# The third weight matrix of a gated MLP converted after the attention instead of during it

## The chip, the cores and the metric

One core of a Trainium2 chip. The metric is the device time of one execution in microseconds (us). The five engines run their own instruction streams: PE (TensorE; PEld is its weight load), DVE (VectorE), ACT (ScalarE), POOL (GpSimd) and SP, which only issues DMAs here. 1% of this kernel's time is 7.9 us.

## The reference, cut to what matters

Three stages, each feeding the next: a masked attention, a gated MLP over all tokens, and a routed mixture of eight experts.

```python
scores = scale * q @ k.T                      # B, H, S, D = 4, 8, 576, 64
scores = where(mask_local if h < 4 else mask_strided, scores, -1e9)
x = softmax(scores) @ v                       # -> 2304 tokens x 512

gate = 1 / (1 + exp(-(x @ w_gate)))           # 512 x 1536
x = (gate * (x @ w_val)) @ w_out              # w_out: 1536 x 512

e_idx = argmax(x @ w_gate2)                   # 8 experts, 512 -> 1024 -> 512
out = x + p * (relu(x @ w1[e_idx]) @ w2[e_idx])   # only where x @ w_skip > 0
...
```

## The kernel before, in words

**Products in three.** Each operand of the large products is held as a high and a low part, and a product is three matmuls (L434 high by high, L435 high by low, L436 low by high). The MLP's weights arrive as 64-bit words. A matrix of a group of 256 hidden columns is two pieces of 512 KB, each fetched by one DMA from SP and converted (`Weights.convert`) by five DVE operations on 128x512 elements (L396, L399, L402, L405, L409), then a copy on ACT that makes the high part (L417), then a subtraction on POOL that makes the low part (L413). The piece's matmuls need both parts. Tiles are named by matrix: `wg`, `wv`, `wo` the raw words, `cvg`, `cvv`, `cvo` the scratch, `whg`/`wlg` and so on the parts. The MLP runs in groups of hidden columns; group 0 is the one that the change touches.

**Attention.** 32 sub-items run as a software pipeline of steps t = 0 to 34. What a step issues, and in which order, is written out by hand as a string of letters, `ORDER`; its first string serves t < 14, the second t = 14 to 32. The letters that matter: S scores (PE L281), e/E exponentials (ACT), I inverse of the sums (DVE L312, L313), n/N normalisation (POOL L319, tile `sm`), f/F transposition (PE L328 of `sm`, evacuated by DVE L330 or ACT L332), A the product with v (PE L342, evacuated by ACT L350/L362 and DVE L351/L364), m/M row maximum (DVE L297), G one piece of filler, L loads. D is `drain(1)`, which issues the next one of the queued conversion operations; a and p issue the ACT copy and the POOL subtraction of a piece whose five operations are done. The raw piece is fetched in the steps listed in `FETCH`, and its conversion is queued two steps later, piece after piece in the order of `early`.

**Filler.** Half products of group 0 for the first three units of 512 tokens (`gv_raw`, six matmuls each, 24 halves) fill PE: one half a step from step `FILL0` on, what is left in the last step.

**The turn.** After the attention its memory is reused by other pools. Then come `glu_raw` of units 0 and 1 (ACT L506 sigmoid, DVE L507 product, ACT L509 copy, POOL L510 subtraction), the gate and value products of unit 3 (`gv(0, 3)`, with ACT L462, DVE L463, ACT L464, DVE L467), and the output products `mout(0, u)`: these alone use `wo` of group 0, three matmuls with its first piece, three with its second, then an ACT copy (L526). `ticks` between them converts the next groups' matrices.

**End of the last group.** At its last unit, `route` is called after each third of the last gate and value products ("g" or "v", kk = 0 to 3) and issues parts of the routing of the unit before: `turn_back` (PE, DVE L738), then the nine small DVE operations of `pick` (L747 to L775), and at ("v", 3) `prep`, which transposes expert 0's first gathered rows (PE L872, ACT L874, DVE L876) for the first expert products (PE L998).

Of the kernel before, what the change touches and what calls it, by code (L numbers as in the profile page):

```python
# [21 lines left out]
def kernel(  # L22
# [25 lines left out]
    G = 2  # L48
# [9 lines left out]
    NU = -(-NT // UT)  # L58
# [114 lines left out]
    def load_qk(b, ty, hp):  # L173
        if hp == 0:
            r = [att.tile([128, 2, 4, 2, D], F32, tag="raw", bufs=4, name=f"raw_{n}{b}{ty}") for n in "qk"]
            r.append(att.tile([128, 2, 2, D], F32, tag="rem", bufs=2, name=f"rem{b}{ty}"))
            raw_t[b, ty] = r
        r = raw_t[b, ty]
        h0 = 4 * ty + 2 * hp
        for i, src in enumerate((q, k)):  # L180
            for h in range(2):
                nc.sync.dma_start(
                    r[i][:, hp, :, h, :], src[b, h0 + h, 0:512, :].rearrange("(p r) d -> p r d", r=4)
                )
        for i, src in enumerate((q, k)):
            nc.sync.dma_start(
                r[2][64 * hp:64 * hp + 64, i], src[b, h0:h0 + 2, 512:S, :].rearrange("h p d -> p h d")
            )
# [234 lines left out]
    after_act, after_pool, glus = [], [], []  # L423

    def flush(jobs):
        todo = list(jobs)
        jobs.clear()
        for job in todo:
            job()

    wt = {}
# [6 lines left out]
    def run(steps, n=99):  # L438
        for _ in range(n):
            if next(steps, 0) == 0:  # L440
                return
# [4 lines left out]
    def gv_mm(g, u, f, nm, tag, step=None):  # L446
        fs = slice(128 * f, 128 * f + 128)
        ps = bank([128, width(u)], tag)
        assert wt[g, nm].ready == 2
        whi, wlo = wt[g, nm].hi, wt[g, nm].lo  # L450
        for kk in range(KD):
            mm3(ps, whi[:, kk, fs], wlo[:, kk, fs], plane(xth[u], kk), plane(xtl[u], kk), kk == 0, kk == KD - 1)
            if step is not None:
                step(nm, kk)
        return ps

    def glu(g, u, f, pg, pvl):
        n = width(u)
        gt = slab2([128, 2, n], F32R, f"gt{g}{u}{f}")
        gts.setdefault((g, u), []).append(gt)  # L460
        sg = late.tile([128, UT], F32, tag="sg", bufs=2, name="sg")[:, 0:n]
        nc.scalar.activation(sg, pg, AF.Sigmoid)  # L462
        nc.vector.tensor_tensor(sg, sg, pvl, op=ALU.mult)  # L463
        nc.scalar.copy(gt[:, 0, :], sg)  # L464

        def low_part():
            nc.vector.tensor_tensor(gt[:, 1, :], sg, gt[:, 0, :].bitcast(F32), op=ALU.subtract)  # L467

        flush(glus)
        if f + 1 < G:  # L470
            glus.append(low_part)
        else:
            low_part()

    def gv_f(g, u, f, step=None):
        glu(g, u, f, *(gv_mm(g, u, f, nm, "ZY"[f], step) for nm in "gv"))

    def gv(g, u):
        for f in range(G):
            gv_f(g, u, f)  # L480

    def gv_raw(u, f, i):
        if i == 0:
            raws[u, f] = slab([128, 2, UT], F32, f"gvr{u}{f}")
        ps = bank([128, UT], "Z")
        w = wt[0, "gv"[i]]
        assert w.ready == 2
        fs = slice(128 * f, 128 * f + 128)
        for kk in range(KD):
            mm3(ps, w.hi[:, kk, fs], w.lo[:, kk, fs], plane(xth[u], kk), plane(xtl[u], kk), kk == 0, kk == KD - 1)  # L490
            if kk == 1:
                yield
        dst = raws[u, f][:, i, :]
        if i == 0:
            nc.vector.tensor_copy(dst, ps)
        else:
            nc.scalar.copy(dst, ps)  # L497
        yield

    def glu_raw(u):  # L500
        for f in range(G):
            raw = raws.pop((u, f))
            gt = slab2([128, 2, UT], F32R, f"gt0{u}{f}")
            gts.setdefault((0, u), []).append(gt)
            sg = raw[:, 0, :]
            nc.scalar.activation(sg, sg, AF.Sigmoid)  # L506
            nc.vector.tensor_tensor(sg, sg, raw[:, 1, :], op=ALU.mult)  # L507
            yield
            nc.scalar.copy(gt[:, 0, :], sg)  # L509
            nc.gpsimd.tensor_tensor(gt[:, 1, :], sg, gt[:, 0, :].bitcast(F32), op=ALU.subtract)  # L510
            yield
# [31 lines left out]
    load_qk(0, 1, 0)  # L543
    load_v(0, 0)
    load_qk(0, 1, 1)
    for nm in "gvo":
        wt[0, nm] = Weights(0, nm, slab, slab)
    ADD = 20
    NRAW = 3
    FILL = {}  # L550
    FILL0 = 13
    BUSY = ((1, 2), (1, 2), (1, 2), (1, 2), (0, 1), (0, 1), (0, 1), (0, 1), (0, 1), (0, 0), (0, 1), (0, 1), (1, 1), (1, 1), (0, 1), (1, 0))
    FETCH = (5, 6, 7, 8, 13, 14)
    halves = [x for u in range(NRAW) for i in range(2) for f in range(G) for x in [gv_raw(u, f, i)] for _ in range(2)]
    for i, x in enumerate(halves):
        FILL.setdefault(min(FILL0 + i, NS + 2), []).append(x)
    early = [(nm, i) for nm in "gvo" for i in range(2)]
    turn(items[0], 0, 8)
    turn(items[0], 1, 1)
    cq = []  # L560
# [59 lines left out]
    def step_loads(t):  # L620
# [16 lines left out]
        if 17 <= t < 23:  # L637
            late_consts(t - 17)
        if t in FETCH:
            nm, i = early[FETCH.index(t)]  # L640
            wt[0, nm].fetch(i)
        if t - 2 in FETCH:
            nm, i = early[FETCH.index(t - 2)]
            cq.append(wt[0, nm].convert(i))
# [7 lines left out]
        "D": lambda t: drain(1), "a": lambda t: flush(after_act), "p": lambda t: flush(after_pool),  # L652
    }
    ps_of = {}
    ORDER = ("eSfEmIFnGaNDTMRpDADL", "SmeEfTIanGNDMRDpLDAF", "GAeEInNfFapDDDD")
    for t in range(NS + 3):
        for c in ORDER[(t >= 14) + (t >= NS + 1)]:
            steps_of[c](t)
# [10 lines left out]
    def slab2(shape, dt, name):  # L669
        return late.tile(shape, dt, tag="slab2", bufs=NSLAB2, name=name)  # L670
# [160 lines left out]
    def init_xs(u):  # L831
        if u == 0:
            zero.append(late.tile([128, TW], F32, tag="row", bufs=8, name="zero"))
            nc.gpsimd.memset(zero[0], 0.0)
            nc.gpsimd.memset(zero[0][:, TW - 1:TW].bitcast(I32), 1 << 16)
        for i in range(3 * u, min(3 * u + 3, NE * SLOTS // 128)):
            nc.sync.dma_start(xs[128 * i:128 * i + 128, :], zero[0])
# [46 lines left out]
    def plan(g, nm):  # L884
        w = Weights(g, nm, slab2, slab3)
        wt[g, nm] = w
        conv.extend([(w, 0), (w, 1)])
# [19 lines left out]
    for g in range(1, NG):  # L907
        for nm in "gvo":
            plan(g, nm)
    todo = [glu_raw(u) for u in range(NRAW)]  # L910
    for n in range(2 * G):
        for u in range(2):
            run(todo[u], 1)
    gv(0, NRAW)
    for u in range(NU):

        def between(d, u=u):
# [7 lines left out]
    for g in range(1, NG):  # L925
        last = g == NG - 1
        for u in range(NU):
            if g == 2:
                init_xs(u)
            if not last:  # L930
                gv_f(g, u, 0)
                if u > 0:
                    mout(g, u - 1, ticks)
                elif g > 1:
                    mout(g - 1, NU - 1, ticks)
                gv_f(g, u, 1)
                continue
            steps = back = picks = iter(())

            def seat(nm, kk):  # L940
                nonlocal steps
                if u > 1 and (nm, kk) == ("g", 1):
                    steps = place(u - 2, rank_sums(rst[u - 2][1], "X"))
                run(steps, 1)

            gv_f(g, u, 0, seat)
            run(steps)
            if u == 0:
                w_e0.append(load_e(0, 0))
            if u == NU - 1:  # L950
                xg, ins = fetch(0, PARTS[:1])
                tc.add_to_no_dep_group("head", ins.ins)
            if u > 0:
                mout(g, u - 1, part(u - 1))
                back = turn_back(u - 1)
                picks = pick(u - 1)
            else:
                mout(g - 1, NU - 1, ticks)

            def route(nm, kk):  # L960
                if u == NU - 1 and (nm, kk) == ("v", 3):
                    pp.extend(prep(0, xg, PARTS[:1], tag="Z", gates=False))
                if nm == "g":
                    run(back, 2)
                else:
                    run(picks, 4)

            gv_f(g, u, 1, route)
            run(picks)
            for i in {0: (1, 2), 1: (3, 4), 2: (5, 6), 3: (7,)}.get(u, ()):  # L970
                w_e0.append(load_e(0, i))
# [15 lines left out]
    pending, jobs = [], []  # L987
# [297 lines left out]
```

## Time and profile before

| | us |
|---|---|
| median of 3 runs | 789.06 (784.98 to 790.59) |
| profiled execution, its own time | 785.84 |
| its span in the trace | 784.1 |

Granted TensorE clock over the span: 0.994 of full speed. The profile is of one execution; the times below are us from the start of its span. Busy time counts no waits. A matmul's start is recorded, its end is modelled, so starts are what is compared.

### The profile page before, as it was taken

What the parts mean: (1) busy time and instruction counts of PE and PEld (TensorE: products, weight loads), DVE (VectorE), ACT (ScalarE), POOL (GpSimd) and SP (SyncE); (2) the same over time, 40 slices, a digit from 0 to 9 for tenths busy, and PEclk for the clock granted to TensorE, in tenths of its full rate; (3) what the DMA queues carried; (4) which work ended last, traced back from release to release, by engine and by line L of the source; (5) the groups of instructions that cost most, each with busy time, mean ns of one, the idle gap of its engine ahead of it and who ended that gap; (6) DMA issues with size and microseconds to landing.
All of it is one profiled execution on the core that took longest, in us unless ns stands there. A gap on an engine that the chain in (4) does not pass through costs nothing. (4 is left out here: it accounts for less than half of the span.)

```text
span 784.1 us, 12866 instructions
## 1 busy us (share of the span) xinstructions
PE 757.9 (97%) x4522; PEld 629.0 (80%) x4524; DVE 487.9 (62%) x1130; ACT 345.2 (44%) x1001; POOL 261.6 (33%) x259
## 2 busy tenths in 40 slices
PE   8989999999999999999999999999999999999994
PEld 5757677688888888888888888888888888888882
DVE  4698876469465574575466457277775776665650
ACT  5877679565211221222111212344444755666530
POOL 5565643253111011011011101424424456665610
PEclk9999999999999999999999999999999999999998
DMA  6988451213101333011002000223346766666600
GB/s 162 212 208 220 105 117 32 81 28 108 54 29 52 110 96 122 28 54 54 27 28 81 28 27 27 71 97 135 109 145 185 254 231 234 233 234 207 215 28 13
DMA packets 86447, 87.82 MB, mean 112 GB/s; under 512 B 55991, under 2 KB 58551, under 8 KB 86376
## 3 DMA queue, kind: packets, MB, share of 16 engines
q1 hardware_dynamic: 81032, 76.45, 32.4%
q0 software_dynamic: 3616, 7.33, 2.7%
q10 hardware_dynamic: 1728, 3.15, 1.1%
q8 instruction: 38, 0.62, 0.4%
q14 instruction: 33, 0.27, 0.1%
HBM read 73.48 MB, written 19.28 MB: 118 GB/s over the span
## 5 line engine op out<-in xcount | busy, mean ns | idle before, releaser
L435 PE MATMUL psX<-gt,who 128*128 128x512 f32 (+1 forms) x240 | 88.4, 369 | 0.0
L434 PE MATMUL psX<-gt,who 128*128 128x512 f32 (+1 forms) x240 | 88.4, 368 | 0.0
L464 ACT CAST gt<-sg 128x512 fp32r<-128x512 f32 (+1 forms) x54 | 30.9, 572 | 130.3 <-DVE sg L463 128.8
L436 PE MATMUL psX<-gt,wlo 128*128 128x512 f32 (+1 forms) x240 | 88.3, 368 | 0.0
L319 POOL TENSOR_TENSOR sm<-sm,rs 96x384 f32<-96x384 f32 (+2 forms) x64 | 51.0, 816 | 66.4 <-DVE rs L313 37.0
L528 DVE TENSOR_TENSOR acc<-psX,acc 128x512 f32<-128x512 f32 (+1 forms) x100 | 62.8, 631 | 11.6 <-PE psX L436 11.4
L463 DVE TENSOR_TENSOR sg<-sg,psZ 128x512 f32<-128x512 f32 (+1 forms) x27 | 17.0, 628 | 67.4 <-PE psZ L436 65.8
L413 POOL TENSOR_TENSOR wlv<-cvv,whv 128x512 fp32r<-128x512 f32 x12 | 17.0, 1415 | 113.9 <-ACT whv L417 113.9
L436 PEld LDWEIGHTS psX<-gt,wlo 128*128 128x128 f32 x240 | 45.2, 188 | 7.6
L434 PEld LDWEIGHTS psX<-gt,who 128*128 128x128 f32 x240 | 45.2, 189 | 7.5
L435 PEld LDWEIGHTS psX<-gt,who 128*128 128x128 f32 x240 | 45.2, 188 | 7.5
L434 PE MATMUL psZ<-xth,whv 128*128 128x512 f32 (+1 forms) x132 | 50.3, 381 | 0.9 <-ACT gvr L497 0.7
L434 PE MATMUL psZ<-xth,whg 128*128 128x512 f32 (+1 forms) x132 | 50.3, 381 | 0.0
L436 PE MATMUL psZ<-xth,wlv 128*128 128x512 f32 (+1 forms) x132 | 49.2, 373 | 0.0
L435 PE MATMUL psZ<-xtl,whv 128*128 128x512 f32 (+1 forms) x132 | 49.1, 372 | 0.0
L436 PE MATMUL psZ<-xth,wlg 128*128 128x512 f32 (+1 forms) x132 | 49.0, 371 | 0.0
L435 PE MATMUL psZ<-xtl,whg 128*128 128x512 f32 (+1 forms) x132 | 49.0, 371 | 0.0
L463 DVE TENSOR_TENSOR sg<-sg,psY 128x512 f32<-128x512 f32 (+1 forms) x27 | 17.0, 628 | 47.9 <-PE psY L436 45.7
L1076 POOL DMA_INDIRECT out_dram<-xg x16 | 21.1, 1321 | 75.1 <-DVE xg L1075 40.4
L413 POOL TENSOR_TENSOR wlo<-cvo,who 128x512 fp32r<-128x512 f32 x12 | 17.4, 1450 | 83.4 <-ACT who L417 83.4
L467 DVE TENSOR_TENSOR gt<-sg,gt 128x512 fp32r<-128x512 f32 (+1 forms) x54 | 34.0, 630 | 17.1 <-ACT gt L464 16.6
L413 POOL TENSOR_TENSOR wlg<-cvg,whg 128x512 fp32r<-128x512 f32 x12 | 18.4, 1531 | 71.8 <-ACT whg L417 55.2
(748 smaller groups left out, 2244.5 us busy)
## 6 DMA issues: line engine op xcount, KB each, us to landing
w1r<-in_moe_w_dram SPq DMA_DIRECT2D x32, 512.0 KB
w2r<-in_moe_w_dram SPq DMA_DIRECT2D x32, 512.0 KB
wg<-in_moe_w_gate_dram SPq DMA_DIRECT2D x12, 512.0 KB
wv<-in_moe_w_val_dram SPq DMA_DIRECT2D x12, 512.0 KB
wo<-in_moe_w_out_dram SPq DMA_DIRECT2D x12, 512.0 KB
raw_q<-in_q_dram SPq DMA_DIRECT2D x32, 128.0 KB
raw_k<-in_k_dram SPq DMA_DIRECT2D x32, 128.0 KB
xs<-zero SPq DMA_DIRECT2D x14, 260.5 KB
```

The costliest lines, as they stand in the source:

```text
L319: nc.gpsimd.tensor_tensor(x, x, rs[:n, h, 0:m].rearrange("p (w o) -> p w o", o=1).to_broadcast([n, m, c]), op=ALU.mult)
L413: nc.gpsimd.tensor_tensor(l, wf, h.bitcast(F32), op=ALU.subtract)
L434: nc.tensor.matmul(ps, lhsT=whi, rhs=xhi, start=start, stop=False)
L435: nc.tensor.matmul(ps, lhsT=whi, rhs=xlo, start=False, stop=False)
L436: nc.tensor.matmul(ps, lhsT=wlo, rhs=xhi, start=False, stop=stop)
L463: nc.vector.tensor_tensor(sg, sg, pvl, op=ALU.mult)
L464: nc.scalar.copy(gt[:, 0, :], sg)
L467: nc.vector.tensor_tensor(gt[:, 1, :], sg, gt[:, 0, :].bitcast(F32), op=ALU.subtract)
L528: nc.vector.tensor_tensor(ac, po, ac, op=ALU.add)
L1076: nc.gpsimd.indirect_dma_start(out=out[:, :], out_offset=bass.IndirectOffsetOnAxis(ap=xg[t][:n, TW - 1:TW].bitcast(I32), axis=0), in_=y, i ...
```

## The change

`wo` of group 0 leaves the attention. Its two pieces are fetched behind the attention, into tiles of the pools that open there, and its ten conversion operations are issued one by one by a callback of the gate and value products of unit 3 (each call also issues the waiting POOL and ACT parts). In the attention a step up to 13 drains two conversion operations instead of three, the four pieces left are fetched at steps 5, 6, 8, 10, the filler starts at step 14 instead of 13, and at the end of the last group `prep` is called at ("v", 0) instead of ("v", 3).

```diff
-    for nm in "gvo":
+    for nm in "gv":
         wt[0, nm] = Weights(0, nm, slab, slab)
...
-    FILL0 = 13
+    FILL0 = 14
...
-    FETCH = (5, 6, 7, 8, 13, 14)
+    FETCH = (5, 6, 8, 10)
...
-    early = [(nm, i) for nm in "gvo" for i in range(2)]
+    early = [(nm, i) for nm in "gv" for i in range(2)]
...
-    ORDER = ("eSfEmIFnGaNDTMRpDADL", "SmeEfTIanGNDMRDpLDAF", "GAeEInNfFapDDDD")
+    ORDER = ("eSfEmIFnGaNDTMRpDAL", "SmeEfTIanGNDMRDpLDAF", "GAeEInNfFapDDDD")
...
     todo = [glu_raw(u) for u in range(NRAW)]
+    wt[0, "o"] = Weights(0, "o", slab2, slab3)
+    for i in range(2):
+        wt[0, "o"].fetch(i)
+    first_o = chain(wt[0, "o"].convert(0), wt[0, "o"].convert(1))
+
+    def turn_o(nm, kk):
+        flush(after_pool)
+        flush(after_act)
+        run(first_o, 1)
+
     for n in range(2 * G):
         for u in range(2):
             run(todo[u], 1)
-    gv(0, NRAW)
+    for f in range(G):
+        gv_f(0, NRAW, f, turn_o)
+    for jobs in (after_act, after_pool):
+        flush(jobs)
...
-                if u == NU - 1 and (nm, kk) == ("v", 3):
+                if u == NU - 1 and (nm, kk) == ("v", 0):
                     pp.extend(prep(0, xg, PARTS[:1], tag="Z", gates=False))
```

Conversion operations that the attention's steps issue: before, three a step in steps 8 to 13 and 2, 1, 3, 3, 3 in steps 14 to 18, 30 in all; after, two a step in steps 8 to 13 and 3, 3, 2 in steps 14 to 16, 20 in all.

DVE around step 12, before. L396 to L409 are the conversion, `cvv` and `wv` the value matrix, the other rows the attention's own:

```order
L399 SCALAR_TENSOR_TENSOR cvv_918<-wv_659,cvv_918 128x512
L330 COPY pT<-psY 128x288
L297 TENSOR_REDUCE mx<-psX 126x2
L312 TENSOR_SCALAR sums<-sums 96x6
L313 RECIPROCAL rs<-sums 96x6
L402 SCALAR_TENSOR_TENSOR cvv_918<-wv_659,cvv_918 128x512
L230 TENSOR_SCALAR kq_983<-psY 128x32x16
L297 TENSOR_REDUCE mx<-psX 126x2
L405 TENSOR_SCALAR wv_659<-wv_659 128x512
L351 TENSOR_TENSOR xtl_381<-psY,xth_379 128x160
L351 TENSOR_TENSOR xtl_922<-psY,xth_920 128x128
L409 SCALAR_TENSOR_TENSOR cvv_918<-wv_659,cvv_918 128x512
```

The same place after (`cvg`, `wg`: the gate matrix):

```order
L312 TENSOR_SCALAR sums<-sums 96x6
L313 RECIPROCAL rs<-sums 96x6
L405 TENSOR_SCALAR wg_583<-wg_583 128x512
L230 TENSOR_SCALAR kq_975<-psY 128x32x16
L297 TENSOR_REDUCE mx<-psX 126x2
L409 SCALAR_TENSOR_TENSOR cvg_834<-wg_583,cvg_834 128x512
L351 TENSOR_TENSOR xtl_381<-psY,xth_379 128x160
L351 TENSOR_TENSOR xtl_916<-psY,xth_914 128x128
```

The conversion operation that stood last in the step, behind L351, is gone, and the conversion as a whole is one matrix further back.

DVE at the turn, before (`gvr` the raw products of `glu_raw`, `sg`/`gt` those of unit 3, the last row the next group's conversion):

```order
L507 TENSOR_TENSOR gvr_1804<-gvr_1804 128x512
L463 TENSOR_TENSOR sg<-sg,psZ 128x512
L463 TENSOR_TENSOR sg<-sg,psY 128x512
L467 TENSOR_TENSOR gt_2525<-sg,gt_2525 128x512
L467 TENSOR_TENSOR gt_2556<-sg,gt_2556 128x512
L396 TENSOR_SCALAR cvg_2579<-wg_2573 128x512
```

and after:

```order
L507 TENSOR_TENSOR gvr_1859<-gvr_1859 128x512
L396 TENSOR_SCALAR cvo_2487<-wo_2457 128x512
L399 SCALAR_TENSOR_TENSOR cvo_2487<-wo_2457,cvo_2487 128x512
L402 SCALAR_TENSOR_TENSOR cvo_2487<-wo_2457,cvo_2487 128x512
L405 TENSOR_SCALAR wo_2457<-wo_2457 128x512
L409 SCALAR_TENSOR_TENSOR cvo_2487<-wo_2457,cvo_2487 128x512
L396 TENSOR_SCALAR cvo_2510<-wo_2459 128x512
L399 SCALAR_TENSOR_TENSOR cvo_2510<-wo_2459,cvo_2510 128x512
L402 SCALAR_TENSOR_TENSOR cvo_2510<-wo_2459,cvo_2510 128x512
L463 TENSOR_TENSOR sg<-sg,psZ 128x512
L405 TENSOR_SCALAR wo_2459<-wo_2459 128x512
L409 SCALAR_TENSOR_TENSOR cvo_2510<-wo_2459,cvo_2510 128x512
```

All ten operations of `wo` now stand behind the last L507, eight of them ahead of the first L463 and two between the two L463.

DVE at the end of the last group, before:

```order
L771 TENSOR_REDUCE rmx<-eq 128x4
L773 TENSOR_TENSOR eq<-eq,rmx 128x32
L775 TENSOR_TENSOR oh_all<-eq,va 128x32
L876 TENSOR_TENSOR xx_6072<-psZ,xx_6072 128x2x128
L876 TENSOR_TENSOR xx_6073<-psZ,xx_6073 128x2x128
L463 TENSOR_TENSOR sg<-sg,psY 128x256
L467 TENSOR_TENSOR gt_6084<-sg,gt_6084 128x256
```

and after:

```order
L876 TENSOR_TENSOR xx_6038<-psZ,xx_6038 128x2x128
L876 TENSOR_TENSOR xx_6039<-psZ,xx_6039 128x2x128
L747 TENSOR_TENSOR lg<-lp 128x40
L759 TENSOR_REDUCE rmx<-lg 128x4
L761 TENSOR_SCALAR va<-lg 128x4
L763 TENSOR_TENSOR eq<-lg,rmx 128x32
L765 TENSOR_TENSOR lm_all<-lg,rmx 128x32
L767 TENSOR_TENSOR eq<-eq,desc 128x32
L771 TENSOR_REDUCE rmx<-eq 128x4
L773 TENSOR_TENSOR eq<-eq,rmx 128x32
L775 TENSOR_TENSOR oh_all<-eq,va 128x32
L463 TENSOR_TENSOR sg<-sg,psY 128x256
```

The two L876, which wait for the gathered rows, now stand ahead of the nine operations of `pick` instead of behind them.

## Rows read from the trace of the kernel before

**Rows 1.** The page's first part: busy us, share of the span, instructions.
```profile
PE 757.9 (97%) x4522; PEld 629.0 (80%) x4524; DVE 487.9 (62%) x1130; ACT 345.2 (44%) x1001; POOL 261.6 (33%) x259
```

**Rows 2.** Busy by stretch: length, PE PEld DVE ACT POOL, clock, DMA, GB/s.
```profile
34.35:60.80 26.45, 22.84 (x230) 16.43 (x228) 23.69 (x60) 20.85 (x97) 16.01 (x17) 1.00 0.89 215
60.80:75.20 14.40, 13.88 (x121) 10.29 (x120) 11.54 (x30) 9.20 (x47) 10.42 (x13) 1.00 0.95 245
75.20:96.80 21.60, 19.67 (x166) 14.67 (x164) 18.23 (x46) 15.98 (x70) 12.07 (x16) 0.92 0.50 117
91.70:95.20 3.50, 3.50 (x18) 2.94 (x17) 2.52 (x13) 2.24 (x13) 2.34 (x4) 0.51 0.01 2
580.00:600.00 20.00, 17.67 (x140) 15.72 (x140) 13.91 (x67) 10.57 (x32) 7.20 (x14) 1.00 0.66 220
```

**Rows 3.** Waits of PE, first 100 us: total, count, median.
```profile
PE psY L328 <- POOL sm L319: 3.2, 5, 1.2
```

**Rows 4.** Busy by stretch, DVE's conversion alone: first tile wg, then tile wo.
```profile
34.35:60.80 26.45, 6.45 (x10) 1.00 0.89 215
75.20:96.80 21.60, 8.06 (x9) 0.92 0.50 117
```

**Rows 5.** PE's timeline: start, us, instruction; steps 3 and 8, then step 13's filler.
```profile
17.09 0.90 PE L281 MATMUL psX<-kq 64*96 64x128 f32 x12
...
34.80 0.90 PE L281 MATMUL psX<-kq 64*96 64x128 f32 x12
...
57.65 0.48 PE L434 MATMUL psZ<-xth,whg 128*128 128x512 f32 x1
...
59.13 0.39 PE L167 MATMUL psY<-busy_in 128*128 128x512 bf16 x1
```

**Rows 6.** PE's timeline at the turn.
```profile
153.40 0.78 PE L342 MATMUL psY<-pT,v 108*64 108x108 f32 x12
...
166.27 0.39 PE L436 MATMUL psX<-gt,wlo 128*128 128x512 f32 x1
```

**Rows 7.** DVE's timeline at the turn and behind it.
```profile
159.53 2.40 DVE L507 TENSOR_TENSOR gvr<-gvr 128x512 f32<-128x512 f32 x2 [1.27 <-ACT gvr L506]
163.17 0.69 DVE L463 TENSOR_TENSOR sg<-sg,psZ 128x512 f32<-128x512 f32 x1 [1.24 <-ACT sg L462]
...
183.35 0.42 DVE L396 TENSOR_SCALAR cvv<-wv 128x512 int32<-128x512 int32 x1
...
185.14 1.53 DVE L405 TENSOR_SCALAR wv<-wv 128x512 int32<-128x512 int32 x1
...
187.32 0.42 DVE L396 TENSOR_SCALAR cvo<-wo 128x512 int32<-128x512 int32 x1
...
194.63 0.69 DVE L409 SCALAR_TENSOR_TENSOR cvo<-wo,cvo 128x512 f32<-128x512 int32 x1
```

**Rows 8.** POOL's timeline behind the turn.
```profile
184.61 1.78 POOL L413 TENSOR_TENSOR wlv<-cvv,whv 128x512 fp32r<-128x512 f32 x1 [2.79 <-ACT whv L417]
...
196.06 1.49 POOL L413 TENSOR_TENSOR wlo<-cvo,who 128x512 fp32r<-128x512 f32 x1 [1.75 <-ACT who L417]
```

**Rows 9.** DVE's timeline at the end of the last group.
```profile
579.54 0.20 DVE L747 TENSOR_TENSOR lg<-lp 128x40 f32<-128x40 f32 x1
...
580.89 0.19 DVE L775 TENSOR_TENSOR oh_all<-eq,va 128x32 bf16<-128x32 f32 x1
...
582.37 0.41 DVE L463 TENSOR_TENSOR sg<-sg,psY 128x256 f32<-128x256 f32 x1
...
583.25 0.43 DVE L467 TENSOR_TENSOR gt<-sg,gt 128x256 fp32r<-128x256 f32 x1 [0.47 <-ACT gt L464]
```

**Rows 10.** PE's timeline at the same place: transposes and first expert product.
```profile
580.33 0.66 PE L872 MATMUL psZ<-ident,xg 128*128 128x128 f32 x4
582.18 0.39 PE L998 MATMUL psY<-xx,w100h 128*128 128x256 f32 x1 [1.20 <-DVE xx L876]
```

**Rows 11.** Tile xg, 560 to 590 us: what its engine idled for before it.
```profile
  DMA xg<-xs: 0.2, 1
```

## The prediction

> **What bounds the kernel now.** I read the page's busy shares first: PE works 97% of the span, 757.9 of 784.1 us [rows 1]. Only what lets PE idle, or runs it at half clock, can be won or lost, some 26 us. So the second view is the busy time by stretch, cut at the steps that the change touches [rows 2]. In steps 8 to 13 (34.35 to 60.80) PE is busy 22.84 of 26.45 us, in steps 14 to 16 13.88 of 14.40, in steps 17 to 20 19.67 of 21.60, and at the end of the last group 17.67 of 20. In the first of these DVE is the busiest engine, 23.69 us, with fixed order and the conversions in it. The waits of PE there name POOL, though: 3.2 us in five waits on the normalisation L319 [rows 3]. POOL's operand comes from DVE's inverses, so a lighter DVE helps only in part. Last I read the timelines at the turn and at the end of the last group [rows 6 to 11], where the change puts new work.
>
> The sum is made against the profiled execution, 785.84 us (784.1 of span and 1.7 around it). The median of the runs is 789.06, 3.2 above; I add these 3.2 at the end.
>
> **Steps 8 to 13.** Eighteen conversion operations become twelve. Ten of them cost DVE 6.45 us there, 0.645 each [rows 4], so six fewer free 3.9 us of DVE. The floor is the pace of steps 3 to 7, which convert nothing: the scores of step 3 start at 17.09, of step 8 at 34.80 [rows 5], 17.71 / 5 = 3.54 a step, 21.3 for six; 26.45 - 21.3 = 5.2 is the most that can go. Nothing goes if POOL sets the pace. The waits on POOL lie between, 3.2, near to DVE's own 3.9; I take -3.3, bounds -5.2 and 0.
>
> **Filler.** Step 13's half takes 57.65 to 59.13 = 1.48 us of PE [rows 5], in a step that DVE sets, so it was free. It now stands at the end, after the attention, where PE has no gap to put it in: +1.5.
>
> **Steps 14 to 16.** Eight operations instead of six: 2 x 0.645 = 1.3 of DVE. But PE idles only 0.5 us in these 14.40 us and DVE has 2.9 us free [rows 2]. Value +0.4, bounds 0 and 1.3.
>
> **Steps 17 to 20.** Nine operations of `wo` leave, 8.06 us of DVE [rows 4]. They were slow there, 0.9 each. PE idles 21.60 - 19.67 = 1.9 us in the stretch and runs 91.70 to 95.20 at 0.51 of its clock, the lower of its two levels, 1.2 GHz [rows 2], which loses 3.50 x 0.49 = 1.7. With DVE at 10 instead of 18 of 21.60 us I take both, -3.6, which is also the most; the other bound is -1.5 (three quarters of the idle time, and the clock as before). What is late next is PE itself.
>
> **The turn.** This is the main price. In the trace PE's first three matmuls of `mout(0, 0)` need the first piece of `wo`, the next three the second, and the sixth, which needs the last low part, starts at 166.27 [rows 6]. Now all ten operations stand on DVE behind the last L507, which ends at 159.53 + 2.40 = 161.93 [rows 7]. A piece took 183.35 to 187.32 = 3.97 from its first operation to the next piece's first, with one operation held up: an L405 of 1.53 us instead of 0.42, while POOL ran L413 from 184.61 to 186.39 [rows 7, 8]. At the turn POOL is busy with L510 in the same way, so I take one held-up operation a piece. Two pieces are 7.9, one L463 between them 0.6 (0.69, overlapping a little): DVE is done at 170.5. Behind the last operation come the ACT copy and the POOL subtraction: from L409's end at 194.63 + 0.69 = 195.32 to L413's end at 196.06 + 1.49 = 197.55 is 2.23 [rows 7, 8]. So the sixth matmul starts at 172.7 instead of 166.27: +6.4. PE's order has nothing else to do meanwhile, and everything that follows it on PE moves by as much. Without a held-up operation each piece is 1.1 shorter, +4.2; with two each, +8.6.
>
> What queues behind the wait: on DVE the two L463 and L467 of unit 3 and then the next group's conversion start some 6 us late, but PE is as late, so nobody waits for them more than before. The fetches cost nothing: 512 KB at the 215 GB/s of [rows 2] is an estimated 2.4 us, the second piece is issued when the attention's last matmul, 153.40 [rows 6], is done, and DVE comes to it after 165.
>
> **PE's clock after the stall.** The trace shows both outcomes. After steps 17 to 20 with 1.9 us of idle time in many pieces the clock fell to 0.51 for 3.50 us, a loss of 1.7; in 580 to 600 PE idled 2.33 us and the clock stayed at 1.00 [rows 2]. The stall of 6 us is longer than either and in two or three pieces. I take one such drop, +1.7; bounds 0 and two drops, 3.4.
>
> The Trainium skill, "TensorE: Matmul & The Clock Gate", section "What's actually happening", says that the throttled state is the default and that activity releases it, so by it an idle PE falls back and pays on its return, which speaks against this change. By that rule the sum stands as it is or grows by another 1.7; if the stretch 580 to 600 is the better model, it is 1.7 smaller. The trace shows cases of both.
>
> **The end of the last group.** The gathered rows land when PE's transposes begin: PE waited 0.2 for them, and the transposes start at 580.33 [rows 10, 11]. Calling `prep` earlier cannot bring them earlier. PE now waits for the rows with three quarters of the value product still ahead, and these fill the 1.20 us that PE waited for L876 [rows 10]; that much is even. But DVE now waits at L876 with the nine operations of `pick` behind it; they ran 579.54 to 581.08, 1.54 us, under that wait [rows 9]. They now run between L876 and L463 (582.37), so L463 and L467 (583.25) come up to 1.5 later, and the last output products wait for them. PE's expert products hide a little: +1.3, bounds 0 and 1.5. A gain is excluded, as the rows' landing sets the place.
>
> **Sum.** -3.3 + 1.5 + 0.4 - 3.6 + 6.4 + 1.7 + 1.3 = +4.4: the profiled execution 790.2, the median 793.5. All lower bounds give -5.2 + 1.5 + 0 - 3.6 + 4.2 + 0 + 0 = -3.1, 786.0; all upper bounds 0 + 1.5 + 1.3 - 1.5 + 8.6 + 3.4 + 1.5 = +14.8, 803.9.
>
> **Rivals.**
> 1. *The attention runs at its floor and the turn is cheap.* Steps 8 to 13 give all 5.2, no DVE operation is held up at the turn (4.2), and the clock stays (0): -5.2 + 1.5 + 0.4 - 3.6 + 4.2 + 0 + 1.3 = -1.4, 787.7. For it: steps 3 to 7 have the same attention work and run at 3.54. Against: the waits name POOL, and POOL's L510 does run where the conversion now stands.
> 2. *DVE and POOL collide at the turn* and the change is slower. Two operations of each piece are held up beside L510 and L413, the stall is 8.6, and the clock falls twice (3.4): -3.3 + 1.5 + 0.4 - 3.6 + 8.6 + 3.4 + 1.3 = +8.3, 797.4. For it: the last pair of L507 took 2.40 where one L463 takes 0.69 [rows 7]. Against: an L405 alone is 0.42, and the rows show one held-up operation in a piece, not two. It decides from a stall of 8.2 on, where the whole passes 1%.
> 3. *The change doesn't do what it says*: with two operations a step the gate matrix is ready so late that step 14's filler waits for a POOL subtraction of 1.78 [rows 8], and the time moved out of the steps comes back as that wait: 793.5 + 1.8 = 795.3. Against: the gate's ten operations are done in step 12.
>
> **How the numbers follow.** The forecast has 0.52, with its own range 788.5 to 796.5; rival 1 has 0.22, rival 2 0.18, rival 3 0.05, and 0.03 is for what I don't see. The range 786.5 to 799.0 takes in rival 1's time and rival 2's and leaves out the two ends of the bounds. 1% is 7.9 us, about what a measurement of this kernel can tell from no change. Faster than 781.2 no case reaches, since the lowest sum is 786.0: 0.04. Slower than 796.95 is most of rival 2, a tenth of the forecast and a part of the rest: 0.19. Within 1%: 0.77.
>
> **What would show it.** In the changed kernel's trace: steps 8 to 13 (first scores to first scores) near 23.2 us instead of 26.45; no half clock before 97; the last L413 of `wlo` ending 6 us after PE's last value product, with PE waiting on ACT `who` and POOL `wlo`; a stretch of half clock behind it; at the end of the last group L463 behind L775 and PE waiting for `gt`. I am wrong if steps 8 to 13 don't shrink (POOL sets them), if PE's waits on `who` and `wlo` add up to under 4 or over 9 us, or if the clock stays at 1.00 behind the turn.

## The result and the profile after

| | us |
|---|---|
| before, median of 12 runs | 785.84 (784.5 to 790.67) |
| changed, median of 12 runs | 791.75 (790.7 to 795.23) |
| ratio | 1.0077, 95% interval 1.0058 to 1.0096 |
| profiled execution of the changed kernel, its span | 789.8 |

The changed kernel is slower by 0.8%. It is within 1%, as forecast, and slower by more than its interval. The spans of the two profiled executions differ by 5.7 us; the forecast for the profiled execution was 4.4.

The page's first part answers to [rows 1]. PE has 2.4 us more to do (the same matmuls, some of them at half clock) and idles 3.3 us more.

```profile
PE 760.3 (96%) x4524; PEld 630.7 (80%) x4524; DVE 490.9 (62%) x1130; ACT 344.7 (44%) x1001; POOL 259.4 (33%) x259
```

Busy time by stretch of the changed kernel, columns as in [rows 2]: steps 8 to 13, 14 to 16, 17 to 20, then a stretch behind the turn and one in the last group.

```profile
34.26:59.24 24.98, 21.48 (x225) 15.62 (x223) 22.15 (x56) 20.06 (x96) 14.23 (x17) 1.00 0.91 219
59.24:73.56 14.32, 13.65 (x119) 10.10 (x118) 12.52 (x27) 9.28 (x47) 8.54 (x11) 1.00 0.89 207
73.56:91.73 18.17, 17.95 (x166) 13.38 (x164) 13.00 (x43) 14.64 (x68) 9.29 (x14) 1.00 0.52 119
167.90:171.30 3.40, 2.94 (x7) 2.36 (x8) 3.36 (x7) 1.74 (x3) 0.41 (x1) 0.51 0.00 0
584.40:587.80 3.40, 3.40 (x18) 3.40 (x18) 1.69 (x9) 0.94 (x3) 0.27 (x3) 0.50 1.07 331
```

Against [rows 2], steps 8 to 13 are 1.5 shorter, 14 to 16 as long as before, 17 to 20 are 3.4 shorter with DVE at 13.0 instead of 18.2 us and no half clock. Two stretches of half clock (1.2 GHz) are new: behind the turn, and in the last group.

PE's timeline of the changed kernel at the turn (start, us, instruction, in brackets the idle time ahead of it and what ended it) answers to [rows 6].

```profile
150.90 0.47 PE L434 MATMUL psZ<-xth,whg 128*128 128x512 f32 x1 [1.69 <-DVE xtl L364]
162.60 0.50 PE L434 MATMUL psX<-gt,who 128*128 128x512 f32 x1 [0.57 <-ACT who L417]
164.14 0.49 PE L436 MATMUL psX<-gt,wlo 128*128 128x512 f32 x1 [0.81 <-POOL wlo L413]
167.00 0.50 PE L434 MATMUL psX<-gt,who 128*128 128x512 f32 x1 [2.37 <-ACT who L417]
168.36 0.79 PE L436 MATMUL psX<-gt,wlo 128*128 128x512 f32 x1 [0.62 <-POOL wlo L413]
```

The four waits for `who` and `wlo` are the stall that was forecast: 0.57 + 0.81 + 2.37 + 0.62 = 4.37. The first row is a wait that was not: 1.69 for the PSUM bank of unit 3's first product. The trace puts it down to DVE's L364, so the bank is one that L364 had to empty first. From the attention's last matmul to the sixth output matmul the changed kernel takes 19.40 us where the kernel before took 12.35, 7.05 more: these five waits, 6.06, and about 1.0 that PE's starts lose around them.

DVE's timeline there, which answers to [rows 7], shows why the stall is as long as it is.

```profile
154.51 2.46 DVE L507 TENSOR_TENSOR gvr<-gvr 128x512 f32<-128x512 f32 x2 [1.27 <-ACT gvr L506]
156.90 1.52 DVE L396 TENSOR_SCALAR cvo<-wo 128x512 int32<-128x512 int32 x1
158.45 1.66 DVE L399 SCALAR_TENSOR_TENSOR cvo<-wo,cvo 128x512 int32<-128x512 int32 x1
...
162.99 1.64 DVE L402 SCALAR_TENSOR_TENSOR cvo<-wo,cvo 128x512 int32<-128x512 int32 x1
164.56 0.67 DVE L463 TENSOR_TENSOR sg<-sg,psZ 128x512 f32<-128x512 f32 x1
...
165.61 0.69 DVE L409 SCALAR_TENSOR_TENSOR cvo<-wo,cvo 128x512 f32<-128x512 int32 x1
```

From 156.90 to 166.30 DVE does `wo` and one L463, 9.4 us, with three operations held up to 1.5 or 1.7 us. POOL was at work beside each of them, with L510 beside the first two and with the first L413 beside the third. The second L413 is what PE's last wait is for:

```profile
153.42 6.13 POOL L510 TENSOR_TENSOR gt<-gvr,gt 128x512 fp32r<-128x512 f32 x4 [12.24 <-ACT gt L509]
162.63 1.46 POOL L413 TENSOR_TENSOR wlo<-cvo,who 128x512 fp32r<-128x512 f32 x1 [3.07 <-ACT who L417]
167.03 1.28 POOL L413 TENSOR_TENSOR wlo<-cvo,who 128x512 fp32r<-128x512 f32 x1 [2.94 <-ACT who L417]
```

At the end of the last group, PE (answers to [rows 10]) waits for the gathered rows in one piece and then works at half clock:

```profile
584.27 1.06 PE L872 MATMUL psZ<-ident,xg 128*128 128x128 f32 x4 [1.37 <-DMA xg<-xs]
...
589.08 0.38 PE L434 MATMUL psX<-gt,who 128*128 128x256 f32 x1 [0.25 <-ACT gt L464]
```

and DVE (answers to [rows 9]) runs `pick` behind L876, so that L463 starts 2.1 after L876, right behind L775. In the kernel before it came 0.7 after L876, at 582.37 [rows 9]. The first row is L876 in the kernel before, the others are the changed kernel:

```profile
581.70 0.76 DVE L876 TENSOR_TENSOR xx<-psZ,xx 128x256 fp32r<-128x256 f32 x2 [0.62 <-ACT xx L874]
...
586.05 0.76 DVE L876 TENSOR_TENSOR xx<-psZ,xx 128x256 fp32r<-128x256 f32 x2 [2.90 <-ACT xx L874]
586.72 0.19 DVE L747 TENSOR_TENSOR lg<-lp 128x40 f32<-128x40 f32 x1
...
588.07 0.19 DVE L775 TENSOR_TENSOR oh_all<-eq,va 128x32 bf16<-128x32 f32 x1
588.17 0.41 DVE L463 TENSOR_TENSOR sg<-sg,psY 128x256 f32<-128x256 f32 x1
```

### The profile page after: what moved, and what is told of

Read it like the earlier page. It is cut to its first block, busy times and chain, and to the rows that moved or that the text cites. A ratio compares the mean times of both kernels' runs of the same rounds, so it can differ in the third digit from the quotient of the medians.

```text
span 789.8 us, 12872 instructions
## 1 busy us (share of the span) xinstructions
PE 760.3 (96%) x4524; PEld 630.7 (80%) x4524; DVE 490.9 (62%) x1130; ACT 344.7 (44%) x1001; POOL 259.4 (33%) x259
## 5 line engine op out<-in xcount | busy, mean ns | idle before, releaser
L464 ACT CAST gt<-sg 128x512 fp32r<-128x512 f32 (+1 forms) x54 | 30.9, 572 | 134.0 <-DVE sg L463 132.5
L319 POOL TENSOR_TENSOR sm<-sm,rs 96x384 f32<-96x384 f32 (+2 forms) x64 | 49.8, 798 | 66.4 <-DVE rs L313 39.9
L463 DVE TENSOR_TENSOR sg<-sg,psZ 128x512 f32<-128x512 f32 (+1 forms) x27 | 17.0, 628 | 66.3 <-PE psZ L436 66.3
L413 POOL TENSOR_TENSOR wlv<-cvv,whv 128x512 fp32r<-128x512 f32 x12 | 16.6, 1382 | 113.9 <-ACT whv L417 113.9
L463 DVE TENSOR_TENSOR sg<-sg,psY 128x512 f32<-128x512 f32 (+1 forms) x27 | 17.0, 629 | 49.1 <-PE psY L436 46.4
L413 POOL TENSOR_TENSOR wlo<-cvo,who 128x512 fp32r<-128x512 f32 x12 | 17.4, 1446 | 89.4 <-ACT who L417 89.4
L413 POOL TENSOR_TENSOR wlg<-cvg,whg 128x512 fp32r<-128x512 f32 x12 | 18.2, 1520 | 72.2 <-ACT whg L417 72.2
```

The costliest lines, as they stand in the source:

```text
L319: nc.gpsimd.tensor_tensor(x, x, rs[:n, h, 0:m].rearrange("p (w o) -> p w o", o=1).to_broadcast([n, m, c]), op=ALU.mult)
L413: nc.gpsimd.tensor_tensor(l, wf, h.bitcast(F32), op=ALU.subtract)
```

## The experiments

Every execution can be cut on PE's timeline into the same pieces: A, the start of the attention's last matmul; B, from there to the sixth output matmul (the first that needs all of `wo`); C, from there to the 101st; D, from the first routing matmul (L734) to the end. From the 101st to the first routing matmul the kernels take 320.8 (e5 and e8 321.2). The table has these pieces from each profiled execution, with the half clock that its clock record shows (`h`, us) in or just before the piece (what fell at the very end is left out, and what fell in the attention: 3.4 at 91.7 in the kernel before, which is in its A, and 3.4 at 42.1 in e10), and the median of the runs beside that of the kernel before on the same chip.

| run | A | B | C | D | median | before |
|---|---|---|---|---|---|---|
| before | 153.92 | 12.35 | 26.88 | 270.18 | 785.84 | |
| changed | 148.96 | 19.40 | 28.38, h 3.4 | 272.24, h 3.4 | 791.75 | 785.84 |
| e1 route back | 148.65 | 19.39 | 29.89, h 6.8 | 270.25 | 790.78 | 785.06 |
| e2 route only | 152.17 | 12.35 | 26.88 | 274.96, h 6.8 | 787.36 | 785.06 |
| e3 wo early | 154.34 | 12.35 | 26.88 | 273.36, h 6.8 | 788.65 | 785.06 |
| e4 wo thin | 152.22 | 15.65, h 3.4 | 26.88 | 271.60 | 788.80 | 785.06 |
| e5 unit 4 first | 148.28 | 21.93 | 22.94 | 271.62 | 788.41 | 785.41 |
| e6 dummies | 149.13 | 20.22, h 3.4 | 26.88 | 275.26, h 10.2 | 791.34 | 785.41 |
| e7 bank | 148.92 | 19.47 | 29.05, h 10.2 | 273.49 | 791.82 | 785.41 |
| e8 three mended | 148.54 | 23.93, h 6.8 | 22.45 | 270.22 | 788.55 | 785.41 |
| e9 changed again | 148.37 | 19.41 | 29.07, h 6.8 | 275.02, h 10.2 | 792.70 | 785.10 |
| e10 wo late only | 151.02 | 19.45 | 29.25, h 10.2 | 269.83 | 791.94 | 785.10 |
| e11 unit 1 later | 149.19 | 16.60 | 29.60, h 3.4 | 271.47 | 789.10 | 785.10 |
| e12 thin, mended | 151.85 | 12.35 | 26.88 | 269.63 | 783.51 | 785.10 |

**Route edit undone (e1), route edit alone (e2).**

```diff
-                if u == NU - 1 and (nm, kk) == ("v", 0):
+                if u == NU - 1 and (nm, kk) == ("v", 3):
```

> The changed kernel with prep back at (v, 3). Theory (each term of the change stands by itself; the route edit costs 2.1 us, since PE waits 1.4 us in one piece for the gathered rows, drops to half clock behind it, and L463 waits behind pick): about 2.1 below the changed kernel, 789.6 where it has 791.75, no half clock between 570 and 610. Rival (the last group's time is set by when the gathered rows land, and moves with everything ahead of it): no difference from 791.75.

> The kernel before with the route edit alone (prep at (v, 0)). Theory: 2.1 above the kernel before, 787.9 where it has 785.84, with a stretch of lower clock behind one wait of about 1.4 us for xg and L463 behind L775. Rival (the edit costs only where the turn has shifted the DMAs): 785.8, within 0.3 of before.

Alone the edit costs 787.36 - 785.06 = 2.3 (ratio 1.0024, 1.0009 to 1.0039); the rival is out. Undone, the changed kernel gains 1.0 where I expected 2.1, and only 0.2 when each median is set against its own runs of the kernel before (5.7 against 5.9 above them). Its ratio of 1.0072 (1.0053 to 1.0090) overlaps that of the changed kernel, so these times don't show a gain. In the trace D is back at 270.25, but this execution had more half clock behind the turn (C 29.89 instead of 28.38), which took most of it back. In e2 PE waits 1.4 for `xg` and 1.0 for L464 (in rows of this kind: total, count, longest; the third number in [rows 3] is the longest too, and not the median):

```profile
PE psZ L872 <- DMA xg<-xs: 1.4, 1, 1.4
...
PE psX L434 <- ACT gt L464: 1.0, 1, 1.0
```

**The changed kernel once more (e9).**

> The changed kernel once more, on this chip and beside the next runs. Theory (the half clock behind the stall at the turn and behind the wait for xg comes in stretches whose length differs from one execution to the next): 791.7 again, its median 0.5 to 1.5 above that of the run with the route edit undone. Rival (that run's smaller gain than 2.1 means the route edit itself costs less): no other stretch of half clock than 178.5 to 182 and 595 to 598 on the trace's own clock, and 2.1 lost between the first gathered rows and the end.

792.70 instead of the expected 791.7, ratio 1.0098 (1.0071 to 1.0125), 1.9 above e1 when each is set against its own runs of the kernel before; the intervals of the two still overlap. The same program has other stretches of half clock this time, longer ones:

```profile
165.40:172.20 6.80, 5.64 (x12) 3.97 (x13) 5.55 (x10) 3.88 (x7) 1.28 (x1) 0.50 0.00 1
595.40:605.60 10.20, 10.20 (x54) 10.11 (x54) 5.62 (x32) 3.66 (x14) 5.93 (x10) 0.50 0.75 231
```

So the route edit has two prices: 1.3 to 1.4 in D without any half clock (e4, e5, e11 against 270.2) and up to 5.1 with it (e6). Of the nine profiled executions with the route edit five have half clock in D, of the five without it none.

**Which part makes the attention shorter: `wo` early again (e3), `wo` late and nothing else (e10).** e3 is the changed kernel with

```diff
-    FETCH = (5, 6, 8, 10)
+    FETCH = (5, 6, 8, 10, 13, 14)
...
-    early = [(nm, i) for nm in "gv" for i in range(2)]
+    early = [(nm, i) for nm in "gvo" for i in range(2)]
```

and none of the work for `wo` at the turn. e10 is the kernel before with only that work at the turn and `early` of "gv".

> The changed kernel with the third matrix back in the attention (fetched at 13 and 14, three operations a step from 14 on, nothing of it at the turn); two operations a step up to 13, filler from 14 and the route edit stay. Theory: the stall at the turn (4.4 of waits for who and wlo, and the half clock behind it, 1.5) goes, and the 3.4 that steps 17 to 20 had gained are lost: 791.75 - 5.9 + 3.4 = 789.3, with the half clock near 92 us back. Rival (the filler's and the two operations' effect carries the attention's gain, the matrix nothing): 791.75 - 5.9 = 785.9, steps 17 to 20 as short as in the changed kernel.

> The kernel before with only the third matrix taken out of the attention and converted at the turn; three operations a step, fetch steps 5 to 8, filler from 13 and prep at (v, 3) as before. Theory (the move gains 3.4 in steps 17 to 20 and costs 7.05 at the turn and 1.5 of clock): 785.4 + 5.1 = 790.5, steps 8 to 13 as before. Rival (it is the two operations a step and the filler that let the attention run 5 us shorter): steps 17 to 20 as before, 785.4 + 8.5 = 793.9.

e3: 788.65 (ratio 1.0038, 1.0021 to 1.0056), e10: 791.94 (1.0092, 1.0070 to 1.0115); both near the theory, e10 1.4 over it, with more half clock than the theory had: 10.2 behind the turn and 3.4 in steps 8 to 13. Busy time by stretch, steps 8 to 13 and 17 to 20, of e3:

```profile
34.58:59.54 24.96, 21.46 (x225) 15.62 (x223) 22.14 (x56) 20.02 (x96) 14.22 (x17) 1.00 0.96 232
...
73.86:96.38 22.52, 18.42 (x166) 13.38 (x164) 21.69 (x47) 16.09 (x70) 13.02 (x14) 1.00 0.50 113
```

and of e10:

```profile
34.41:61.62 27.21, 24.32 (x230) 17.40 (x228) 23.70 (x60) 20.92 (x97) 16.02 (x17) 0.94 0.87 216
...
76.00:93.88 17.88, 17.88 (x166) 13.38 (x164) 10.93 (x37) 15.02 (x68) 6.59 (x12) 1.00 0.42 102
```

They part the two gains cleanly. Two operations a step make steps 8 to 13 25.0 long whether `wo` is early or late; with three they are 27.2 in e10 (clock 0.94) and 26.45 in the kernel before. `wo` gone makes steps 17 to 20 17.9 long where it is 22.5 with it, and DVE's 21.7 of 22.5 us in e3 shows what sets that. In e3 twelve conversion operations run in this stretch (ten of `wo` and two left over of `wv`), in the kernel before nine.

How much `wo` costs there in the kernel before is told by e2, whose attention is the same program. No half clock fell in its attention; steps 17 to 20 took 20.0 instead of 21.6 us, with the same work of DVE, and A is 152.17 instead of 153.92:

```profile
74.98:95.02 20.04, 18.10 (x166) 13.38 (x164) 18.21 (x46) 16.01 (x70) 10.92 (x14) 1.00 0.55 123
```

So of the 3.4 us that steps 17 to 20 became shorter, 1.6 are the half clock that fell in the one profiled execution of the kernel before, and 1.9 to 2.2 are there without it (20.0 against 18.2 and 17.9). Of the three executions that convert `wo` there at three operations a step one had half clock in these steps; of the nine that convert it at the turn none had.

**What the stall at the turn is (e5, e6, e7).** e5 puts unit 4's products ahead of the first output product:

```diff
-    for f in range(G):
-        gv_f(0, NRAW, f, turn_o)
+    for u in (NRAW, NRAW + 1):
+        for f in range(G):
+            gv_f(0, u, f, turn_o)
...
-        if u + NRAW + 1 < NU:
-            gv(0, u + NRAW + 1)
```

e6 adds 20 matmuls into the first output product's bank, which that product overwrites; e7 reserves a bank, with `bank([128, UT], "X")` in front of `todo`.

> The changed kernel with the gate and value products of unit 4 (48 matmuls of 256 columns, some 5.6 us of PE) ahead of the first output product instead of behind it; the conversion at the turn stays where it is. Theory (the stall is PE's order: it stands at who and wlo with other work behind it): the waits for who and wlo, 4.4 us together, fall to under 1, and the half clock behind them, 1.5, goes: 791.75 - 4 - 1.5 = about 786.3. Rival (the conversion's DVE and POOL time is on the path whatever PE does, because unit 4's products need DVE behind it too): no gain, 791.5.

> The changed kernel with 20 matmuls of 512 columns added ahead of the first output product, into its PSUM bank, which the first product then overwrites: 4.5 us of PE work put where PE waits for who and wlo, to no use. Theory (the half clock behind the stall is caused by the stall, and costs 1.1 to 2.6): the sixth matmul stays near 168.4, the granted clock between 160 and 175 is 1.00 instead of 0.89, and the time falls by 1.5 to 790.2. Rival (the clock falls whatever PE does there, or its cost is made up later): 791.75 or more, up to +4.5 should the dummies not fit into the wait.

> The changed kernel with one PSUM bank reserved ahead at the turn, so that the first product of unit 3 gets a bank that was freed earlier and no longer waits 1.69 us for DVE's L364. Theory (at the turn the conversion on DVE ends last, and the wait for the bank lies beside it): the wait goes, PE stands longer at who and wlo instead, time the same, 791.7 within 0.5. Rival (the two waits add up): 1.7 lower, 790.0.

e5 falls to 788.41 (ratio 1.0052, 1.0033 to 1.0070), between theory and rival. The waits for `who` and `wlo` are gone and the clock stays, but others come:

```profile
PE psX L434 <- ACT acc L526: 1.1, 3, 0.5
PE psZ L434 <- ACT sg L462: 1.0, 1, 1.0
...
PE psZ L434 <- DVE sg L463: 0.5, 1, 0.5
```

and in the stretch from the seventh to the 101st output matmul DVE is busy 21.19 of 22.71 us:

```profile
170.44:193.15 22.71, 21.76 (x95) 17.12 (x94) 21.19 (x29) 12.78 (x24) 8.72 (x6) 1.00 0.28 93
```

The ten operations moved behind the attention must be done there beside the next groups' conversion. PE's stall had hidden this; with the stall filled DVE is nearly full, and part of the gain comes back as waits for what DVE and ACT deliver. The 101st output matmul starts at 193.15, where the kernel before has it too: the whole gain of the attention is used up there.

e6 shows the clock. With PE kept at work the stall's half clock is gone: C is 26.88, as before. The same stretch in the changed kernel and in e6:

```profile
162.00:175.00 13.00, 8.63 (x33) 6.34 (x32) 10.20 (x17) 7.62 (x14) 4.91 (x4) 0.87 0.00 1
162.00:175.00 13.00, 13.00 (x65) 10.98 (x64) 11.10 (x17) 6.98 (x13) 4.12 (x3) 1.00 0.00 1
```

B is 0.8 longer than in the changed kernel (20.22): this execution had 3.4 of half clock behind the wait for the bank, so the dummies began some 1.6 later than they would have and ended behind the conversion. The median of 791.34 (ratio 1.0077, 1.0055 to 1.0098) can't be told from the changed kernel's; the cause is shown by the trace, its worth in time is not.

e7 takes the wait for the bank away and nothing is gained, as the theory had it (791.82, ratio 1.0083, 1.0060 to 1.0105). PE stands longer for `who` instead:

```profile
PE psX L434 <- ACT who L417: 4.4, 2, 2.3
```

(the changed kernel has 2.9), and B is 19.47 against 19.40. DVE's conversion ends last at this turn, and the bank lay beside it. D holds a wait of 1.8 in this execution for which the profile shows no cause.

**What stands ahead of the conversion (e11).** `glu_raw` of unit 1 goes behind unit 3's products:

```diff
-    for n in range(2 * G):
-        for u in range(2):
-            run(todo[u], 1)
+    run(todo[0])
     for f in range(G):
         gv_f(0, NRAW, f, turn_o)
+    run(todo[1])
```

> The changed kernel with glu_raw of unit 1 behind the conversion of the third matrix instead of ahead of it, so that only two of the four L507 and L510 stand ahead. Theory (what stands ahead of the conversion on DVE, and POOL's L510 beside it, set the stall): the conversion starts near 153.2 instead of 156.9 with at most two held-up operations, the sixth matmul near 164 instead of 168.4, and the time falls to between 786.2 (nothing comes back) and 788.2 (DVE's work behind the turn comes back as PE's waits up to 200 us, as in the run with unit 4's products ahead, where the 101st output matmul started at 193.15). Rival (the second piece's fetch, which waits for the attention's last matmul, sets the stall): 791.7, the sixth matmul near 168.

789.10 (ratio 1.0057, 1.0035 to 1.0079). The first operation of `wo` starts at 155.41 instead of 156.90, two are held up instead of three (L396 and L399, which POOL's L510 no longer meets, take 0.41 and 0.69), and B falls from 19.40 to 16.60; the sixth matmul is at 165.79, between theory and rival. In C some 1.2 come back. So what stands on DVE ahead of the conversion, and POOL beside it, do set the stall, but the gain is smaller than I said, and the time lies 0.9 above the theory's upper end: L507 waits for ACT's L506, which I had left out.

```profile
154.14 1.35 DVE L507 TENSOR_TENSOR gvr<-gvr 128x512 f32<-128x512 f32 x1 [1.27 <-ACT gvr L506]
155.41 0.41 DVE L396 TENSOR_SCALAR cvo<-wo 128x512 int32<-128x512 int32 x1
```

**Looking for a better version (e4, e8, e12).** e8 is the changed kernel with the edits of e1, e5 and e7. e4 is e3 with one operation a step in steps 17 to 20 and two from 21:

```diff
-    FETCH = (5, 6, 8, 10, 13, 14)
+    FETCH = (5, 6, 8, 10, 14, 15)
...
-    ORDER = (..., "SmeEfTIanGNDMRDpLDAF", "GAeEInNfFapDDDD")
+    ORDER = (..., "SmeEfTIanGNDMRDpLDAF", "SmeEfTIanGNMRDpLAF", "SmeEfTIanGNDMRpLDAF", "GAeEInNfFapDDDD")
...
-        for c in ORDER[(t >= 14) + (t >= NS + 1)]:
+        for c in ORDER[(t >= 14) + (t >= 17) + (t >= 21) + (t >= NS + 1)]:
```

and e12 is e4 with the edits of e1 and e7.

> As the one before, but the third matrix is converted thinly in the attention: one operation a step in steps 17 to 20, two from 21. Theory (DVE load in steps 17 to 20 sets PE's idle time and the half clock there; from step 21 on PE is full and the operations are hidden): no stall at the turn, and of the 3.4 of steps 17 to 20 at least 2 stay: 791.75 - 5.9 + 1 = about 786.9, or 784.8 were the route edit undone as well. Rival (any operation of the third matrix in the attention costs its DVE time on the path, 0.645 each): 791.75 - 5.9 + 6.5 = 792.3.

> The changed kernel with three edits: prep back at (v, 3), unit 4's products ahead of the first output product, and the bank of the run before. Theory (the attention's gain of 5 us stays, the turn costs under 1 us once PE has other work and its bank, the last group is as before): 785.06 - 5 + 1.5 = about 781.5, below both kernels. Rival (the turn's conversion delays the DVE work behind it and comes back as waits later): 785 or more.

> The third matrix thinly in the attention (one operation a step in steps 17 to 20, two from 21), two operations a step up to 13, filler from 14, prep at (v, 3) and the reserved bank at the turn. Theory (the route edit is worth 2.1 and the wait for the bank with the half clock behind it 3.2, since nothing of DVE ends later there): 788.8 - 2.1 - 3.2 = 783.5, about 2 below the kernel before. Rival (the bank's wait is covered as at the changed kernel's turn): 786.7, no faster than before.

e4 came to 788.80 (1.0036, 1.0021 to 1.0051), 1.9 over the theory: the wait for the bank stands there with nothing of DVE's behind it to hide it, and its execution had 3.4 of half clock after it (B 15.65 instead of 12.35). The runs of e4 lie in two groups, five at 788.8 to 789.2 with the profiled one among them, and four at 786.7 to 787.0, where the theory was; no trace shows the second group. e8 stayed at 788.55 (1.0044, 1.0028 to 1.0060): the rival. DVE's work for `wo` came back as one wait of 2.8,

```profile
PE psZ L434 <- ACT sg L462: 2.8, 1, 2.8
```

with half clock around it. e12 has none of these and its median is below that of both kernels: 783.51, ratio 0.9982 (0.9971 to 0.9994) to the kernel before. B, C and D are those of the kernel before or less, and A is 2.1 earlier. Busy time of steps 8 to 13, 17 to 20, and from there to the attention's last matmul:

```profile
34.03:58.97 24.94, 21.45 (x225) 15.61 (x223) 22.10 (x56) 20.01 (x96) 14.21 (x17) 1.00 0.93 221
...
73.30:92.18 18.88, 18.07 (x166) 13.37 (x164) 16.79 (x47) 14.66 (x68) 10.76 (x14) 1.00 0.58 140
92.18:151.85 59.67, 56.96 (x490) 42.80 (x490) 39.86 (x196) 43.43 (x188) 25.62 (x41) 1.00 0.30 78
```

Steps 17 to 20 take 18.88 instead of 18.17 in the changed kernel and 20.04 in e2. The last row is where e12 pays: the changed kernel takes 57.23 there and e2 57.15, so two operations a step from step 21 on cost 2.4 to 2.5 us, where e4's theory had them hidden. Against e2, the kernel before's attention without half clock, A is only 0.3 earlier (151.85 and 152.17). The other 1.75 of the 2.1 are the half clock of that one execution. The runs point the same way: the lowest of e12 is 783.07, the lowest of the kernel before beside it 783.11, but the twelve of e12 end at 783.92 and those of the kernel before reach 788.88. What e12 wins is mostly that it is steady; that half clock is what the other runs of the kernel before lose by isn't shown, as they have no trace.

## Why the prediction was right

The forecast of +4.4 for the profiled execution came out at +5.7, and that of 793.5 for the median at 791.75. With more runs the median of the kernel before came down from 789.06 to 785.84, so the 3.2 that the sum had added for the median of three were too much, and the +4.4 stands against +5.9 in the medians. That 793.5 came so near to 791.75 is in part luck: 3.2 too much and 1.5 too little.

| term | forecast | measured in the two traces | from |
|---|---|---|---|
| steps 8 to 13 | -3.3 | -1.5 | 24.98 - 26.45 |
| filler half at the end | +1.5 | +0.1 | A less the shift at step 21 (-5.07 to -4.96) |
| steps 14 to 16 | +0.4 | -0.1 | 14.32 - 14.40 |
| steps 17 to 20 | -3.6 | -3.4 | 18.17 - 21.60 |
| stall at the turn | +6.4 | +7.05 | B |
| clock behind it | +1.7 | +1.5 | C |
| end of the last group | +1.3 | +2.1 | D |

- *Steps 17 to 20 and the turn* were right in place, cause and size. e3 and e10 show that the gain belongs to `wo` alone, and e5, e7 and e11 that DVE's order at the turn sets the stall. The sum's two parts in steps 17 to 20, 1.9 of idle time and 1.7 of clock, are what the runs show: 1.9 to 2.2 and 1.6. But e2 shows that the second part is not there in each execution of the kernel before, so it is a price of the execution that was profiled. Which operations are held up was wrong: not L405, but L396, L399 and L402, and three in all instead of two.
- *Steps 8 to 13 and the filler* are the mis-sized pair, and their errors offset each other: -1.8 forecast, -1.4 measured. The step that was mis-sized is "eighteen operations become twelve": that is what the steps issue, but DVE ran only sixteen of them in the stretch before and twelve after (60 and 56 DVE instructions in the rows). So four left it, not six, DVE's busy time fell by 1.5 (23.69 to 22.15) instead of 3.9, and the stretch by as much. Waits of PE for POOL's L319 remain, 1.6 us in two waits between 34 and 92. The filler half at the end was nearly free, because PE idled in the last steps: 1.6 us in 138.00 to 154.10 of the kernel before, 0.8 in the same part of the changed one (second row).

```profile
138.00:154.10 16.10, 14.47 (x105) 10.33 (x104) 6.94 (x33) 8.41 (x33) 3.91 (x6) 1.00 0.32 99
133.00:149.00 16.00, 15.22 (x110) 11.20 (x106) 6.78 (x29) 8.27 (x33) 3.69 (x6) 1.00 0.12 34
```

- *The clock* fell once behind the stall for 3.4, as the forecast took it. In five executions with the stall as it is (the changed kernel, e1, e7, e9, e10) it fell for 3.4 to 10.2 us there, and C was 1.5 to 3.0 over that of the kernel before. In e6, where PE had the dummies, it did not fall there. By the Trainium skill, "TensorE: Matmul & The Clock Gate", section "What's actually happening", throttled is the default state and activity releases it; e6 agrees, with C at 26.88 once PE was active.
- *The last group's* mechanism was right (L463 behind L775, 1.3 to 1.4 where the clock stays), but I left out that the wait for the gathered rows now comes in one piece, 1.37 us, behind which the clock fell for 3.4; that is most of what was missing.
- *Not seen:* the wait of 1.69 for the bank. It cost nothing in the changed kernel (e7), and 3.3 with the half clock behind it in e4.

Rival 1 failed in steps 8 to 13, which did not reach their floor, and at the turn. Rival 2 failed because the stall was 7.05, under its 8.2, and in the changed kernel's profiled execution the clock fell once behind it; in e7, e9, e10 and e1 it fell for two or three times as long. Rival 3 did not occur: no wait of step 14's filler is in the trace.

## What to carry to other kernels

Work that is taken off an engine near its limit is worth the gap it closes, but look where it lands: a conversion moved to a place where PE needs its result at once costs its whole chain, and once that wait is filled the same engine's load comes back a little later. Spreading the ten operations thinly (e12) cost nothing at the turn, but from step 21 on it gave back most of what the steps ahead had gained. Before a gain is credited to a change, see whether half clock fell in the execution that it is measured against: it made 1.6 to 1.75 of the 5 us by which the attention became shorter here. Size a new wait of PE as the wait and the half clock behind it, and look at several executions before reading one.

## What the runs showed of the hardware

One program shows stretches of half clock of different lengths: the changed kernel 3.4 us at the turn and 3.4 in the last group in one execution, 6.8 and 10.2 in another (e9), and its span went from 789.8 to 792.7. At the turn both stand at the same waits. In the last group the first began with the end of the wait for the gathered rows (584.3), the second at 595.4, 11 us behind it and behind two shorter waits of PE, 1.00 and 0.42. DVE operations on two operands of SBUF (L399, L402) took 1.64 to 1.66 instead of 0.69 beside POOL's subtractions and L396 took 1.52 instead of 0.42, while an L463 that reads PSUM took 0.69 in the kernel before beside an L510. The wait of 1.7 us for a PSUM bank behind the attention stands in the changed kernel and not in e10, which asks for the same banks there, and one tile asked for ahead took it away (e7); that the two kernels were given different banks is inferred from the wait.
